# RWKV-6 attention and a leaky-ReLU feed-forward on one core: more transposes by DMA, stores behind the loads, a new written order

## The chip, the core and the metric

The kernel runs on one core of a Trainium2 chip. The metric is device time in microseconds (us), the median of several executions; lower is better. The core has five engines that run side by side and meet only at semaphores: TensorE (PE) multiplies matrices, VectorE (DVE) and GpSimd (POOL) do elementwise work, ScalarE (ACT) does activations and copies, SyncE (SP) issues most of the data transfers (DMAs). A DMA that an engine issues is carried out by 16 DMA engines, and every engine takes its own instructions strictly in their written order.

## The reference

```python
# r, k, v, w: (4, 8, 768, 48) float32;  u: (8, 48)
for t in range(S):
    cur = einsum('bhd,bhe->bhde', u * k[t], v[t])
    y[t] = einsum('bhd,bhde->bhe', r[t], state + cur)
    state = w[t][..., None] * state + einsum('bhd,bhe->bhde', k[t], v[t])
x = y.transpose(0, 2, 1, 3).reshape(3072, 384)
h = x @ w_in                      # w_in: (384, 2048)
out = maximum(0.01 * h, h) @ w_out  # w_out: (2048, 384), out: (3072, 384)
```

The first part is a linear attention with a decaying state; the second is a feed-forward on its 3072 output rows.

## The kernel before

**Tiling.** The 4 batches of 768 rows are cut into 24 chunks of 128 rows. A chunk n goes through these steps, whose names are used below:

- four loads `ld` of w, k, r and v (192 KB each, SP, line 516), of which w is logged on ACT (`decay`);
- `cum` on PE: the running sum of the logs (L737, L742), then `ci` on DVE and two exponentials on ACT;
- two products, r and k each times an exponential, into one tile `rk` (`product`);
- `turn`: the transpose of `rk` into `rkT`. For chunks outside `TDMA` it is 2 times 4 PE transposes (L441) with one PSUM copy each on DVE or ACT; for chunks in `TDMA` it is one DMA transpose that SP issues (L431);
- `scores` on PE (L787), masked on DVE (L459); `outer` (L798) and the new state s (L479), which takes the decayed old state sb (POOL or DVE, `shrink`);
- `bonus`: ru, ruk (POOL or DVE), a reduction dg (DVE), and vs = v times dg (POOL or DVE);
- `intra` on PE (L817, L822), the sum y on DVE (L490), and `finish`: the transpose of y into `xT`, again by 3 PE transposes (L504) and a copy, or by one DMA transpose (L496).

The first four chunks are done two at a time (`pair`). The feed-forward of a chunk is 4 steps `up` (12 matmuls each, L860), 4 activations g on ACT (L907), 4 steps `down` (4 matmuls each, L928), a copy o out of PSUM (ACT or DVE) and a store of 192 KB (L968). The feed-forward weights are loaded in 16 pieces (L363) and cast to bf16 on DVE, ACT and POOL.

**Buffers.** Inputs and raw weights share a ring `in` of 11 tiles of 128 x 1536 floats, taken in turn; output tiles come from a ring `o` of 4. Attention scores use two PSUM banks (`se`, `so`), the `up` steps two (`hp`), the `down` steps two (`op`).

**Order.** Nothing is scheduled at run time. The kernel lists about 1060 steps with an engine, a duration and the steps they wait for, and `Plan.order` replays them to find an order in which they are written into the engines' queues. The string `EARLY` names every step by number, with a letter where a step goes to another of its allowed engines. In each engine's queue its order is binding; DMA steps it ranks only, so the replay may move a transfer past others. The constant `TDMA = range(12, NCH)` says which chunks are transposed by DMA. During the first 24 us of the replay, gaps on PE are filled with matmuls on zeros (L991).

Of the kernel before, what the change touches and what calls it, by code (L numbers as in the profile page):

```python
# [2 lines left out]

# [9 lines left out]
AX = mybir.AxisListType  # L13


class Plan:
# [23 lines left out]
    def order(self):  # L40
        n = len(self.eng)
        users = [[] for _ in range(n)]
        left = [len(d) for d in self.deps]
        for i, d in enumerate(self.deps):
            for j in d:
                users[j].append(i)
        ready_at = [0.0] * n
        start, done = [None] * n, [0.0] * n
        free = {e: 0.8 for e in self.ENGINES}
        coming = {e: [] for e in self.ENGINES}  # L50
        ready = {e: [] for e in self.ENGINES}
        dma_free = 0.0
        flying = []
        for i in range(n):
            if not left[i]:
                heapq.heappush(coming[self.eng[i]], (0.0, i))
        events = [(0.8, e) for e in self.ENGINES]
        heapq.heapify(events)
        count = 0
        while events:  # L60
            now, e = heapq.heappop(events)
            if free[e] > now + 1e-9:
                continue
            while coming[e] and coming[e][0][0] <= now + 1e-9:
                _, i = heapq.heappop(coming[e])
                heapq.heappush(ready[e], (self.pri[i], i))
            if not ready[e]:
                if coming[e]:
                    heapq.heappush(events, (coming[e][0][0], e))
                continue  # L70
            _, i = heapq.heappop(ready[e])
            start[i] = now
            count += 1
            free[e] = now + self.dur[i] * (1.8 if e == "PE" and now < 8 else 1)
            if self.wire[i] is None:
                done[i] = free[e] + self.LAT[e]
            else:

                flying = [x for x in flying if x[0] > free[e]]
                while sum(x[1] for x in flying) + self.rows[i] > 3300:  # L80
                    free[e] = max(free[e], flying.pop(0)[0])
                dma_free = max(dma_free, free[e]) + self.wire[i]
                done[i] = dma_free + 1.7
                flying.append((done[i], self.rows[i]))
            heapq.heappush(events, (free[e], e))
            for j in users[i]:
                left[j] -= 1
                same = self.eng[j] == e and self.wire[i] is None
                ready_at[j] = max(ready_at[j], free[e] if same else done[i])
                if not left[j]:  # L90
                    f = self.eng[j]
                    heapq.heappush(coming[f], (ready_at[j], j))
                    heapq.heappush(events, (max(ready_at[j], free[f]), f))
        assert count == n, (count, n)
        self.start, self.done = start, done
        return sorted(range(n), key=lambda i: (start[i], i))


class Ring:
# [7 lines left out]
    def take(self):  # L107
        self.n += 1
        k = self.n % len(self.tiles)
        old, self.steps[k] = self.steps[k], []  # L110
        return Use(self.tiles[k], old, self.steps[k])

# [14 lines left out]
def kernel(  # L127
# [11 lines left out]
    nc = tc.nc  # L139
    B, H, S, D = r.shape  # L140
    L = 128
    C = S // L
    NCH = B * C
    NP = H // 2
    DM = H * D
# [6 lines left out]
    TDMA = range(12, NCH)  # L152
# [4 lines left out]
    PWIRE, WIRE, WWIRE = 1.53, 1.15, (1.12, 1.12)  # L157
# [4 lines left out]
    EARLY = """  # L162
        0 4 2 1 3 5 8 58 7 13 6 61 12 32v 36 17 11 16 22 33 120 14 21 30 19 37 18 20 24 15 59 10a 23 26
        9 27 31v 28 40 25 60 29a 38 41a 51 34 39 63 44 53 114 62 42 116 45 65a 66 118 121 64 67 122 46
        35 43 71 68 124 47 126 52 74 73 69 96 48 70 128 76 49 75p 72 136 50v 132 79 115a 78 54 91 80 81
        117 130 83 55 77p 82v 56 84a 721 119 134 92 57 85 722 723 86v 138 87 123a 93 95 725 724 97 125p
        98v 727 726 146 127p 729 99 728 88v 100 129 94 731 89 730 102 137p 140 732 733 101 735 133 148
        90 103 734 131 107 736 104 741 135p 144 109 105 742 106v 139a 142 747 108 737 147 150 110 738
        152 141p 178 743 111 153 112 748 304 744 162 113v 754 167 166 155 168 145v 749 154 753 156 750
        143p 149 739 158 163v 179 157p 755 740 759 164 756 180 160 159 182 762 760 184 209 306 745 763v  # L170
        161 185 765 764 746 151v 169 181 187 165v 751 199 761 189p 198 186 170 171 766 752 172 768 302
        173 757 208 188 174 758 192 210 200v 770 193 774 175 183a 239 194v 190 176 775 767 191a 195v 769
        211 177 196 201 779 197 202 212 237 777 780 203 214 771 224 271 778 215 204 217 781 225v 253 303
        772 783 216 205 219p 270 787 782 218 206 784 226 220 213 222 238 241 207v 790 227 221 223 229
        243 269 285 788 232 244 228 789 301 785 230 245 794 786 231 286 773 793 240 246 247 791 795 248p
        334 287 257 801 254v 258 792 259 796 333 273 255 233 251 317 797 275 234 272 249 252 804 276 318
        305 235 250 807 277 256v 397 289 810 290 236 260 279 278 422 799 811v 242a 280p 307 262 261 800
        366 802 264 337 281 319 815 803 291 335 308 805 282a 274 263 322 808 396 309 320 310 311 265 283
        321 288 798 806 818 266 367 284 339 312p 267 395 821 809 340 292 268v 353 341 824 349 365 294
        354 342 813 825v 350 776 313 295 293 814 816 479 344p 314a 296 315 829 343 817 476 323 297 351  # L180
        316 819 408v 368 399 381 324 820 298 832 409 369 423 326 835 327 299 345 382 371 300 410 822 420
        346a 372 827 823 383 325 336 347 386 433 373 830 328 374 375 329 826 831 355 838 449 376 385 836
        828 448 425 348v 839 401 330 370 843 837 402 812 481 331 846 424 384 332v 404 356 338v 477 844
        403 352 359 451 480 357 833 405 406p 845 398 379 360 426 834 850 358 387 452 840 841 427 851 421
        361 380v 377 429 849 362 438 407 437 378 428 852 842 430 388 450 363 853 847 389 453a 454 411
        505 390 400a 857 848 455 860 364 863 465 431 434 854 456 533 855 457 391 435 466 459p 856 858
        436v 432 871 859 392 412 461 506 458 393 864 394 415 462 478 482 413 865 414 874 416a 463 861
        483 464 504 872 862 439v 417 485 866 418 494 487p 869 493 559 484 440 867 441 870 419 517v 877
        873 558 880 444 518 460 885 443 881 489 888 519 507 508 486 875 490 442 510 532 878 876 511 467
        445 491 879 891 492v 521 488 894 562 522 446 534 886 513 895v 512 515p 469 883 887 472 468 514  # L190
        495 884 892 447 470 509a 899 520 516 893 471 889 868 536 584 473 890 538 902 474 642 539 496 497
        550 905 499 540 475 545 908 549 542 541 896 900 498 583 546 909 564 500 897 901 543p 565 524 898
        547 501 523 906 566 527 567 903 526 560 907 569p 913 502 904 916 882 644a 503 525 911 544 528
        919 585 551 912 922 535 587 917 923 927 568 611 918 571v 914 925 572v 915 589 529 926 573 920
        590 586 552 530 601 921 941 554 531 596 592 928 553 561 591 930 537 613 600 548v 929 933 593 944
        615 670 594 936 570 588a 617 597v 931 937 934 932 598 555 574 938 935 563v 939 595 556 599 942
        910 940 618 557 576 947 624 943 924 672v 612 945 629 619 639 950 620 621 946 948 614 579a 575
        949 602 955 578 628 958 951a 577 961 580 964 581 952 953 965a 582 604 956 954 607 625 667 603
        622 957 959 606 630 962 623 643 960 626 641 645 969 605 963 640 627 972 646 608 616v 647 970 609
        657 648 967 610 971 632 975 697 671 635 656 978 968 658v 669 631 979a 973 634 652 696 983 974  # L200
        649 986 633 650p 668 673 653v 976 981 674 977 651 636 654 675 989 637 708 676 992 966 684 677
        685 638 982 660 680 984 993 695 997 709v 980 655 985 994 987 698 663 681 990 678 988 1000 686v
        991 679 659 1003 682 661 683 1006 662 998 699 1007 995 999 710 1008 701 664 996 702 1004 665 713
# [824 lines left out]
```

## Time and profile before

| | us |
|---|---|
| median of 8 runs | 186.35 (185.99 to 187.03) |
| the profiled execution | 187.03 |
| its span, first to last instruction | 184.9 |
| PE busy / DVE / ACT / POOL | 175.9 / 123.1 / 121.5 / 93.6 |
| mean share of the 16 DMA engines on the queue of the transfers | 85.8% |
| granted TensorE clock | 0.997 |

The profile is of one execution, which was the slowest of the eight. Busy time of PE counts a matmul from its start to a modelled end, and matmuls overlap, so the distance between the starts of consecutive matmuls is the better measure of how fast PE runs. "In 40 slices" means that the span is cut into 40 equal parts, and each digit is the busy share of a part in tenths. SPq rows are the time in which SP issues a transfer, not the transfer itself.

### The profile page before, as it was taken

Reading aid. Unit: us, or ns where it says so; the run is one execution under the profiler, and the core shown is the slowest. Engines: PE = TensorE matmul, PEld = TensorE weight load, DVE = VectorE, ACT = ScalarE, POOL = GpSimd, SP = SyncE. Lnnn points to the kernel's source line nnn. Section 1 sums busy time; section 2 is a strip of 40 time slices with the busy share of each in tenths; the row PEclk is TensorE's granted clock in tenths of the full one; section 3 lists DMA queues with packets and bytes.
Section 4 is the critical chain, followed back from the end, with each engine's and each line's share of the span. In section 5 each row is a group of like instructions: output and inputs, shape, how many; then the busy total and the mean of one; then the engine's idle time right before and its main releaser. Section 6 shows DMA issues by size and latency. Waiting matters only on the chain.

```text
span 184.9 us, 6227 instructions
## 1 busy us (share of the span) xinstructions
PE 175.9 (95%) x2579; PEld 136.9 (74%) x2583; DVE 123.1 (67%) x237; ACT 121.5 (66%) x263; POOL 93.6 (51%) x129
## 2 busy tenths in 40 slices
PE   7987789999999999999999999999999999999992
PEld 2465687777788697788688787886968777877882
DVE  2488585368678877987868778657648589775000
ACT  2784965665786987798958586667657645652660
POOL 7987582552376778787365666313516157220000
PEclk9999999999999999999999999999999999999998
DMA  5999999988989799979997998778986979941202
GB/s 145 261 282 312 350 330 274 264 158 211 214 169 237 142 222 211 195 188 220 134 199 144 144 197 179 191 143 171 182 199 155 196 150 211 205 104 44 66 4 85
DMA packets 120239, 34.62 MB, mean 187 GB/s; under 512 B 109842, under 2 KB 120211, under 8 KB 120211
## 3 DMA queue, kind: packets, MB, share of 16 engines
q1 hardware_dynamic: 120208, 34.22, 85.8%
q8 instruction: 20, 0.33, 0.7%
q14 instruction: 9, 0.07, 0.1%
q10 hardware_dynamic: 2, 0.00, 0.0%
HBM read 25.17 MB, written 4.72 MB: 162 GB/s over the span
## 4 chain that ended last, share of the span: by engine, by line
PE 77%; SPq 11%; DMA 7%; DVE 1%; issue 1%; ACT 1%; POOL 1%; DVEq 0%
PE op L928 31%; PE hp L860 31%; SPq L363 6%; SPq L516 5%; DMA in<-in_moe_w_out_dram 4%; PE se L787 3%; DMA in<-in_r_dram 2%; PE yp L822 2%; PE cp L737 2%; PE yp L817 2%; PE yp L798 2%; PE so L441 1%; PE yp L504 1%; PE se L441 1%; PE cp L742 1%
## 5 line engine op out<-in xcount | busy, mean ns | idle before, releaser
L907 ACT ACTIVATE g<-hp 128x512 bf16<-128x512 f32 x96 | 56.8, 596 | 34.4 <-PE hp L860 32.6
L860 PE MATMUL hp<-xT,w_in_b 128*128 128x128 bf16 x1152 | 76.1, 219 | 1.5 <-ACT w_in_b L329 0.8
L860 PEld LDWEIGHTS <-w_in_b 128*128 128x128 bf16 x1152 | 67.4, 98 | 6.5 <-ACT w_in_b L329 1.2
L928 PE MATMUL op<-w_out_b,g 128*128 128x384 bf16 (+1 forms) x380 | 71.4, 324 | 0.2 <-DVE w_out_b L331 0.2
L928 PEld LDWEIGHTS <-g 128*128 128x128 bf16 x392 | 34.8, 98 | 18.0 <-DVE w_out_b L331 0.3
L334 POOL TENSOR_TENSOR ru<-in,ub 128x384 f32<-128x384 f32 x19 | 19.2, 1012 | 13.3 <-DMA in<-in_r_dram 11.4
L334 POOL TENSOR_TENSOR vs<-in,dg 128x384 f32<-128x384 f32 x19 | 16.5, 875 | 16.1 <-DVE dg L416 8.4
L334 POOL TENSOR_TENSOR rk<-in,ek 128x384 bf16<-128x384 f32 x15 | 15.2, 1015 | 14.2 <-ACT ek L393 12.8
L490 DVE TENSOR_TENSOR y<-yp,vs 128x384 bf16<-128x384 f32 x24 | 13.3, 554 | 12.9 <-PE yp L822 9.3
L334 POOL TENSOR_TENSOR ru<-ru,in 128x384 f32<-128x384 f32 x15 | 15.6, 1045 | 6.0 <-DMA in<-in_k_dram 4.4
L334 POOL TENSOR_TENSOR sb<-s,a 128x384 bf16<-128x384 f32 x13 | 11.3, 868 | 9.9 <-DVE s L479 4.7
L459 DVE TENSOR_TENSOR m<-se,maskb 128x512 bf16<-128x512 f32 x20 | 13.7, 684 | 3.2 <-PE so L787 2.9
L459 DVE TENSOR_TENSOR m<-so,maskb 128x512 bf16<-128x512 f32 x20 | 13.7, 683 | 3.0 <-PE so L787 3.0
L383 ACT ACTIVATE lw<-in 128x384 bf16<-128x384 f32 x24 | 12.3, 519 | 3.7 <-DMA in<-in_w_dram 3.7
L752 DVE TENSOR_TENSOR ci<-cp,lw 128x384 f32<-128x384 f32 x20 | 11.0, 552 | 4.2 <-PE cp L742 4.0
L334 DVE TENSOR_TENSOR rk<-in,cp 128x384 bf16<-128x384 f32 x22 | 12.0, 547 | 2.3 <-ACT cp L393 1.9
L416 DVE TENSOR_REDUCE dg<-ru 128x8 f32<-128x384 f32 x24 | 13.0, 544 | 0.2
L329 ACT COPY o<-op 128x384 f32<-128x384 f32 (+1 forms) x16 | 7.5, 471 | 6.5 <-PE op L928 5.1
L479 DVE TENSOR_TENSOR s<-yp,sb 128x384 f32<-128x384 f32 x14 | 7.7, 553 | 5.2 <-PE yp L798 5.2
L393 ACT ACTIVATE cp<-cp 128x384 f32<-128x384 f32 x22 | 10.5, 478 | 0.6 <-DVE ci L752 0.3
L393 ACT ACTIVATE ek<-ci 128x384 f32<-128x384 f32 x20 | 10.4, 518 | 0.4 <-DVE ci L752 0.2
L775 ACT ACTIVATE a<-cp 64x4 f32<-64x4 f32 x34 | 5.7, 167 | 4.2 <-DVE ci L752 2.0
(125 smaller groups left out, 225.4 us busy)
## 6 DMA issues: line engine op xcount, KB each, us to landing
out_dram<-o SPq DMA_DIRECT2D x23, 192.0 KB, 2.9
in<-in_w_dram SPq DMA_DIRECT2D x20, 192.0 KB, 4.2
in<-in_r_dram SPq DMA_DIRECT2D x20, 192.0 KB, 4.1
in<-in_k_dram SPq DMA_DIRECT2D x20, 192.0 KB, 4.0
in<-in_v_dram SPq DMA_DIRECT2D x20, 192.0 KB, 4.0
in<-in_moe_w_in_dram SPq DMA_DIRECT2D x8, 384.0 KB, 7.6
in<-in_moe_w_out_dram SPq DMA_DIRECT2D x8, 384.0 KB, 7.4
in<-in_w_dram SPq DMA_DIRECT2D x2, 384.0 KB, 5.0
```

Source lines behind the costliest of these rows:

```text
L334: (nc.vector if e == "DVE" else nc.gpsimd).tensor_tensor(out=o, in0=a, in1=b, op=ALU.mult)
L363: "SP", 0.45, lambda part=part, src=src: nc.sync.dma_start(out=part, in_=src), pri,
L383: lambda: nc.scalar.activation(out=lw.t[:, :, 0:D], in_=wn.t, func=AF.Ln),
L393: "ACT", 0.5, lambda: nc.scalar.activation(out=out.t[:], in_=i, func=AF.Exp, scale=scale),
L416: lambda: nc.vector.tensor_reduce(out=dg.t[:], in_=ru.t[:], axis=AX.X, op=ALU.add),
L459: lambda par=par: nc.vector.tensor_tensor(out=m.t[:, par], in0=gt(sc[par].t), in1=mask.unsqueeze(1).to_broadcast([128, NP, 128]), op=ALU.m ...
L490: lambda: nc.vector.tensor_tensor(out=y.t[:], in0=hd(yp.t[:, 0:DM]), in1=vs.t[:], op=ALU.add),
L516: "SP", 0.45, lambda: nc.sync.dma_start(out=view(use), in_=src), P0 + 0.1 * i,
L752: lambda: nc.vector.tensor_tensor(out=ci.t[:], in0=hd(cp.t[:, 0:DM]), in1=lw.t[:, :, 0:D], op=ALU.add),
L860: nc.tensor.matmul(hp.t[:, a * N : (a + 1) * N], lhsT=w_in_b[:, t, (j + a) * 128 : (j + a + 1) * 128], rhs=xT[:, t, c0 : c0 + N], start=(a ...
L907: lambda hp=hp, g=g, j=j, J=J, N=N: nc.scalar.activation(out=g.t[:, j : j + J, 0:N], in_=hp.t[:, 0 : J * N].rearrange("p (a n) -> p a n", ...
L928: nc.tensor.matmul(t[:, 0 : n1 - n0], lhsT=g.t[:, j, off : off + 128], rhs=w_out_b[:, j, n0:n1], start=(j == 0), stop=(j == NJ - 1))
```

## The change

The change does six things.

1. The first 230 steps keep their order on every engine. From there on a new string `ORDER` gives the order of all steps; it is binding for transfers too, and `Plan.order` no longer chooses, it only reckons times for the PE fillers. 70 steps change engine, among them 7 loads and 6 stores that now leave from ACT instead of SP.
2. r and k are transposed by DMA from chunk 9 (before from 12), y from chunk 8 (before from 12). This removes 24 PE transposes of r and k with 6 copies, and 12 of y with 4 copies; it adds 3 DMA transposes of `rk` and 4 of y.
3. The copies o of chunks 4 to 23 go into parts of the input tiles 6 to 10 (four outputs to a tile), each of which is used once. Chunks then take their inputs from 6 tiles in a circle, not from 11. In the new order 12 more of the stores than before come after the last load.
4. In the last chunk the `down` matmuls of the left 256 columns and of the right 128 columns are done in two passes (`quarters`).
5. POOL's vs runs as two instructions of 4 heads each (`by_heads`) from chunk 4 on; the w_in casts read and write in an order of 128 columns at a time (`even`).
6. Planned durations are edited; these act through the number of fillers alone, since the order is written out.

```diff
-    TDMA = range(12, NCH)
+    TDMA = range(9, NCH)
+    YDMA = range(8, NCH)
+    OLATE = 21
...
-    EARLY = """
-        0 4 2 1 3 5 8 58 7 13 6 61 12 32v 36 17 11 16 22 33 120 14 21 30 19 37 18 20 24 15 59 10a 23 26
...
+    ORDER = """
+        0 4 2 1 3 5 8 58 7 6 13 61 32v 36 12 17 11 16 22 33 120 14 21 30 19 37 18 20 24 15 59 10a 23 26
...
+    pair_slots = iter((0, 1, 2, 3))
+    weight_slots = iter((4, 5, 6, 7, 8, 9, 10, 0))
+    chunk_slots = cycle((1, 2, 3, 4, 5, 0))
...
+    def out_tile(ch):
+
+        if ch < 4:
+            return o_r.take()
+        slot, i = divmod(ch - 4, 4)
+        use = in_r.use(6 + slot)
+        return View(use, use.t[:, i * DM : (i + 1) * DM])
...
+        def queue(e):
+            return nc.sync if e == "SP" else nc.scalar
+
...
+        def even(t, which):
+
+            return t if which else t.rearrange("p t (a f) -> p a t f", a=2)
...
+        def by_heads(e, o, a, b, parts):
+            for i in range(parts):
+                hs = slice(i * H // parts, (i + 1) * H // parts)
+                times(e, o[:, hs, :], a[:, hs, :], b[:, hs].unsqueeze(2).to_broadcast([128, H // parts, D]))
...
-                "POOL", 0.92,
-                lambda e: times(e, vs.t[:], vn.t, dg.t[:].unsqueeze(2).to_broadcast([128, H, D])),
-                P0 + 2, reads=[vn, dg], writes=[vs], deps=[vl, s_dg], DVE=0.84)
+                "POOL", 0.88,
+                lambda e: by_heads(e, vs.t, vn.t, dg.t, 2 if e == "POOL" and P0 >= 40 else 1),
+                P0 + 2, reads=[vn, dg], writes=[vs], deps=[vl, s_dg], DVE=0.68)
...
-            if n in TDMA:
+            if n in YDMA:
...
-                "SP", 0.45, lambda: nc.sync.dma_start(out=view(use), in_=src), P0 + 0.1 * i,
-                writes=[use], wire=wire, rows=1024, deps=[cums[n - AHEAD]] if n >= AHEAD else [])
+                "SP", 0.62, lambda e="SP": queue(e).dma_start(out=view(use), in_=src), P0 + 0.1 * i,
+                writes=[use], wire=wire, rows=1024, deps=[cums[n - AHEAD]] if n >= AHEAD else [],
+                **({"SP": 0.62, "ACT": 0.47} if n >= 4 else {}))
...
-            slot = in_r.take()
+            slot = in_r.take(next(chunk_slots))
...
+        def quarters(op, g, off, which):
+            for part, q in which:
+                t, n0, n1 = last_parts(op)[part]
+                for j in range(q * NJ // 4, (q + 1) * NJ // 4):
+                    nc.tensor.matmul(
+                        t[:, 0 : n1 - n0], lhsT=g.t[:, j, off : off + 128], rhs=w_out_b[:, j, n0:n1],
+                        start=(j == 0), stop=(j == NJ - 1))
...
-                    o = o_r.take()
+                    o = out_tile(ch)
...
-                        lambda o=o, ch=ch: nc.sync.dma_start(
+                        lambda e, o=o, ch=ch: queue(e).dma_start(
                             out=rows[ch], in_=o.t[:]),
-                        5, reads=[o], deps=[s_o], wire=0.55, rows=128)
+                        5 if ch >= OLATE else 300, reads=[o], deps=[s_o], wire=0.55, rows=128, SP=0.48, ACT=0.47)
```

The two orders, decoded into step names for the transfers of chunks 9 and 10 and of the last chunks (`T` is a DMA transpose of `rk`, `yT` of y, `st` a store, `@A` issued from ACT):

```
before: ... ldk13 T12 ldr14 ldk16 st8 ldk17 T13 ldr16 ldr15 ldw16 ldk18 yT12 ldw18 T14 ...
before: ... ldw23 st17 st18 ldv23 T22 st19 yT21 T23 st20 yT22 yT23 st21 st22 st23L st23R
after:  ... ldk14@A ldv13 ldv10 T9 ldw14 yT8 T10 ldr12 ldv15 ldv14 T11 yT9 ldw15 ldk15 ldr13 ldv12 T12 yT10 ...
after:  ... ldk23 ldv21 T21 st17@A T22 yT20 st2 st3 st10 st7 st11 st13 st0 st9 st18@A st4 st15 yT21 T23 st19@A st20 yT22 yT23 st21 st23L st22@A st23R
```

## The prediction

> **What bounds the kernel now.** I read the page's busy rows first, then the busy time by stretches, then the chain of work that ended last, and last the instructions of PE in order of time.
>
> ```profile
> PE 175.9 (95%) x2579; PEld 136.9 (74%) x2583; DVE 123.1 (67%) x237; ACT 121.5 (66%) x263; POOL 93.6 (51%) x129
> ...
> PE   7987789999999999999999999999999999999992
> ```
>
> PE is busy from the sixth slice (28 us) to the end. The stretches say the same: between 43 and 158 us nothing but PE is full, and the mean DMA share is near its end too.
>
> ```profile
> 43.00:85.00 42.00, 42.00 (x599) 33.49 (x598) 34.50 (x64) 32.56 (x77) 29.30 (x34) 1.00 0.93 197
> 85.00:158.00 73.00, 72.93 (x1024) 57.49 (x1022) 53.59 (x97) 48.95 (x109) 34.99 (x38) 1.00 0.91 178
> 158.00:182.00 24.00, 23.67 (x334) 19.63 (x332) 8.65 (x16) 12.45 (x24) 1.66 (x2) 1.00 0.38 77
> ```
>
> The columns after the first sum are PE, PEld, DVE, ACT, POOL, clock, DMA share, GB/s. A busy PE need not be a PE at its peak, so I take the chain, where the pieces follow without a hole:
>
> ```profile
> 97.67 1.34 PE hp L860 x24
> 99.01 0.20 PE yp L822 x8
> 99.21 0.65 PE op L928 x4
> 99.86 0.67 PE hp L860 x12
> ...
> 146.79 0.58 SPq L516
> 147.42 4.59 DMA in<-in_r_dram
> 152.10 0.56 DVE rk L334
> ```
>
> An `up` step takes 0.67 us and a `down` step 0.65 wherever they stand. The last three lines are one of the few places after 43 us where the chain leaves PE, for a load; PE itself waited only 0.23 us there. To size what PE loses in all, I give each PE step the median distance from its start to the next step's. From the `up` step at 42.9 us to the end of the last matmul at 181.7 that is 137.3 us, against 138.6 really gone by: all stalls of that stretch come to 1.4 us. So the end is set by how much work PE has, once the weights are there. Before 30 us PE stands still for 9.6 us (matmul starts again), for loads and weight casts.
>
> Here a rule of the Trainium skill speaks against the change. "Perfetto Trace Analysis", section "Identifying the Most-Contended Engine", calls the busy share of matmuls a bad measure and wants that of the weight loads. That is 74%, which would leave PE a quarter of the span in reserve, and work taken off PE would bring 0. By the distances of starts it brings its full length. The distances are measured here, and I go by them.
>
> **The change, part by part.**
>
> *PE transposes removed.* Their cost is the distance to the next step:
>
> ```profile
> 77.25 0.33 PE L504 MATMUL yp<-ident,y 128*128 128x128 bf16 x3
> 77.42 0.39 PE L441 MATMUL se<-ident,rk 128*128 128x128 bf16 x4
> 77.64 0.33 PE L737 MATMUL cp<-lw,trev 128*128 128x384 bf16 x1
> ```
>
> 0.17 us for the three of y, 0.22 for four of r or k. Six groups of four (chunks 9 to 11) and four groups of three (8 to 11): 6 x 0.22 + 4 x 0.17 = 2.0 us, all on the path. The ten copies that go with them (6 on ACT, 4 on DVE) free 3.2 and 1.6 us of engines that are not the bound: 0.
>
> *DMA transposes added.* The 12 of each kind in the trace:
>
> ```profile
> L431 SPq DMA_TRANSPOSE rkT<-rk x12: 1232/1554/3566, 85.5 to 163.4; - x12
> ...
> DMA to landing us min/median/max: 3.1/4.1/5.6
> ```
>
> A transpose of y takes 1.20 to issue and 2.9 to land. A chunk's `rkT` thus comes some 4 us after the products, where the PE way needs 0.39 on PE and 0.58 for the copy at best. "VectorE: DVE Perf Modes", section "The three transpose paths", makes it worse: 1309 ns for a 128x128 block by DMA against 390 on TensorE, with the rule to take TensorE where the result may go to PSUM. For the 36 blocks moved that would be 36 x 0.92 = +33 us if it stood in line. The trace has eight blocks of `rk` landing in 4.1 us, so half a microsecond each, and what they cost depends on what is put between. Adding up PE's durations over the decoded new order gives, from `cum` to `scores`, 12.7, 12.0 and 11.8 us for chunks 9, 10 and 11; chunks that go by DMA now have 8.3 to 21 there, with hardly a stall. From `intra` to the first `up`, chunks 8 to 11 get 5.5 to 8.6; chunks 22 and 23 live on 4.5 and 5.0 now. Covered: 0. Without that cover chunk 9 alone would hold PE by up to 3 us.
>
> *Transfers moved.* By packets in the trace, a load takes 1.0 us of the 16 engines (80.5 us for 80 loads' worth), a pair of transposes 1.70 + 0.64 (28.1 us for 12 pairs), a store 0.55. Seven transposes add 3 x 1.70 + 4 x 0.64 = 7.7 us to the whole. Ahead of the last load, however, stand 12 `rk` and 12 y transposes where there are 10 and 9 now (+3.4 + 1.9), and 7 stores instead of 19 (-6.6): the last load comes after 1.3 us less of transfers than now. SP issues 7 transposes more (3 x 1.55 + 4 x 1.20 = 9.4 us) and 13 other transfers fewer (about 8): it ends even. Ten stores stand in a row ahead of chunk 21's y and chunk 23's r, k; at 0.55 each they fill 5.5 us that PE needs for its steps up to `intra` of chunk 21, about 9 us after the stores can begin. Cost 0; without that cover, up to 1 us.
>
> *ACT as an issuer.* Thirteen issues. The one DMA that ACT issues now took 0.53 us, a load on SP 0.43 to 3.1[...]. 13 x 0.5 = 6.5 us on ACT, which loses 2.8 us of other work and is 66% busy. Behind an issuing ACT stand the g activations, and behind these PE, with two `hp` banks as cover. From below -0.3 (SP's queue moves on earlier), from above four issues of 1.5 us past a cover of 0.7 = +3. I take 0, near the one row.
>
> *Six input tiles for eleven.* A load of chunk n must wait for vs and the products of chunk n-6 on SP, with all later transfers behind it. Before 85 us SP now waits for buffers about 6 us in all. I expect 4 us more, not on PE's path as long as the transposes of `rk` keep their lead: -0 to +2, taken 0.
>
> *POOL's split, casts, last chunk, fillers.* 14 vs in two halves: nothing to 0.2 us each (a small POOL memset takes 0.10), 1.4 us in all, POOL is idle half of the time. The w_in cast on DVE (0.95 us, one of them) may change by 0.3 either way: -0.3 to +0.3. The last chunk's matmuls are the same in sum (2.7 us); its last-but-one store is now chunk 22's 192 KB from ACT instead of 64 to 128 KB from SP: 0 to +0.3. The 15 fillers may become more or fewer, each 0.43 us, in a stretch where PE idles: -0.4 to +0.4. Together taken as +0.1.
>
> *Sum.* -2.0 + 0.1, and for new small stalls +0.1, since the products and transfers are timed less evenly: -1.8. The profiled execution took 187.03; that makes 185.2. It was the slowest of eight, 0.7 above the median of 186.35, where the same difference gives 184.5.
>
> **The rivals.**
>
> *Transfers become the bound (slower).* In the new order chunk 17's `rk` transpose has 85 us of transfers from the end of the w load of chunk 5 (64 loads, 9 + 8 transposes, a store, at the prices above), and a PE without stalls wants it at 126. From 33 us, with some 3 us of weights still in flight and 1.7 for landing, 88 us remain: a pace of 0.97 is needed. Between 44 and 85 us SP got 35 loads and 6 stores through in 40.9 us, a pace of 0.94, its 6 us of waits included, 1.09 without. At 0.94 the transpose is 2.4 us late, and PE, whose `scores` are next in line, stops. Every transpose after it is then late as well:
>
> ```profile
> 85.53 3.57 SPq L431 DMA_TRANSPOSE rkT<-rk  x1
> ...
> 92.11 2.01 SPq L431 DMA_TRANSPOSE rkT<-rk  x1
> ```
>
> shows that the first DMA transpose can hold SP for 3.6 us, and the packets of some transposes run four times longer than others. With one such hold more (1.5 us over the usual) the lag is 3.9 us: -2.0 + 3.9 gives 188.2. For it: SP is one queue and the tiles are six. Against it: after 85 us SP spends about 10 of each 25 us waiting for data, not for transfers, so that the transfers are not the limit there. It decides from a pace below 0.95.
>
> *Part of the gain is eaten.* Single late products (DVE gets 2.3 us of work net, just where it is 80% busy) or ACT's issues stall PE 1.5 to 2 us: 186.1.
>
> *The early order isn't really unchanged.* The v load of chunk 9 stands two places later on SP, and the fillers are counted anew. If the first stretch gains or loses one load's 1 us, the result is 183.5 or 185.5. ACT's long issues belong on the far side: 187.
>
> **How the numbers follow.** PE bound as reckoned, 183.3 to 185.5: 0.58. Part eaten, 185.5 to 186.9: 0.14, of which 0.04 is still faster by over 0.3%. Transfers bound: 0.21, 187 to 190. ACT's issues or six tiles beyond the cover: 0.07, 187. A run of this kernel can tell about 0.3% (0.56 us) from no change. Faster 0.62, same 0.09, slower 0.29. The range for 8 in 10 goes from 183.2 to 187.9, which leaves out the worse half of the transfers' case and the best of the first; the likeliest case alone is 183.3 to 185.5.
>
> **What would show it.** Right: about 36 fewer PE matmuls, the `up` steps still back to back from 43 us on, no L787 or L860 with idle time before it for a transpose, the last matmul near 180. Transfers as the bound: PE waits of 0.5 us and more ahead of `scores` of chunks 12 to 19, and the chain going through SPq L431 and SPq L516. ACT: long ACTq rows with g right behind. I'd be wrong on the sizing if PE's start distances lengthened without any wait.

## The result, and the profile after

The changed kernel takes 191.05 us (median of 11 runs, 189.4 to 195.6) against 186.35 before (185.86 to 187.09): 1.0214 times the time, with a 95% interval of 1.0194 to 1.0234. The prediction was 184.5 us, faster. The ratio leaves out four runs of 193 to 196 us, in which TensorE's mean clock was 0.978 or 0.979 where it was 0.991 or 1.0 in the others; what lowers the clock is part of what follows, but none of these four has a profile.

The profiled execution took 190.67 us (span 188.8). From its page, the row of PE and that of TensorE's clock:

```profile
PE 178.3 (94%) x2549; PEld 138.2 (73%) x2552; DVE 124.6 (66%) x243; ACT 113.4 (60%) x245; POOL 96.9 (51%) x145
...
PEclk9999999999999999999997899999999999999999
```

The trace has 30 matmuls fewer, and yet PE is busy for 2.4 us more. The 7 and 8 in the clock's row, at 99 to 108 us, are the reason: part of the work ran at half speed. The busy times by stretches (after the first sum: PE, PEld, DVE, ACT, POOL, clock, DMA share, GB/s):

```profile
43.00:85.00 42.00, 41.64 (x589) 32.85 (x587) 35.61 (x68) 29.18 (x67) 30.92 (x40) 1.00 1.01 183
85.00:158.00 73.00, 70.87 (x968) 56.04 (x967) 53.58 (x99) 42.56 (x96) 37.52 (x49) 0.98 0.98 183
158.00:182.00 24.00, 22.75 (x327) 18.99 (x325) 8.33 (x15) 12.11 (x23) 0.83 (x1) 1.00 0.40 126
```

Before, the middle stretch held 72.93 us of PE work at clock 1.00; now 2.1 us of it are empty and the mean clock is 0.98. PE's last matmul ends at 185.1 us in place of 181.7, with the `up` step that the prediction counted from at 42.6 in place of 42.9: 142.6 us for what took 138.8. The view of waits names the two largest holes, and who stood behind the second:

```profile
ACT g L924 <- DMA out_dram<-in: 2.3, 1, 2.3
PE se L796 <- DMA rkT<-rk: 1.9, 1, 1.9
PE op L949 <- ACT g L924: 1.4, 2, 1.2
```

**First hole.** SP's own instructions and PE's, in order of time (start, duration; idle time before in brackets):

```profile
90.05 0.58 SPq L524 DMA_DIRECT2D in<-in_r_dram  x1
90.68 1.40 SPq L524 DMA_DIRECT2D in<-in_w_dram  x2
92.18 1.72 SPq L504 DMA_TRANSPOSE xT<-y  x1
94.00 0.53 SPq L524 DMA_DIRECT2D in<-in_k_dram  x1
94.63 2.00 SPq L439 DMA_TRANSPOSE rkT<-rk  x1
...
98.32 0.78 PE L869 MATMUL hp<-xT,w_in_b 128*128 128x128 bf16 x11
100.96 0.23 PE L796 MATMUL se<-rkT 48*128 48x128 bf16 x1 [1.86 <-DMA rkT<-rk]
```

The products of chunk 13 were ready at 89.5. Its transpose (the row at 94.63) stood in SP's queue behind the w loads of chunks 16 and 17, y's transpose of chunk 11 and the k load of chunk 18, whose data were first used at 123.4. It was issued 5.1 us after it could have been, took 6.3 us to land, and PE stood still for 1.86 us. It is none of the added transposes: before, chunk 13 went by DMA too. It was issued at 92.11 us there (a row that the prediction shows), and its `scores` came 8.4 us later, without a wait:

```profile
100.46 0.23 PE L787 MATMUL se<-rkT 48*128 48x128 bf16 x1
```

In the changed kernel the clock then went to half for 3.41 us; these are the two steps of the clock's record on either side of 101.45 us:

```profile
98.04:101.45 3.41, 1.55 (x29) 1.22 (x27) 2.29 (x5) 1.72 (x5) 1.53 (x2) 1.00 1.24 196
101.45:104.86 3.41, 3.41 (x27) 2.73 (x26) 2.52 (x5) 1.08 (x2) 3.13 (x4) 0.50 0.84 163
```

The second has PE busy throughout, with half the matmuls for the time: 1.7 us lost with no wait shown.

**Second hole.** ACT and PE around 160 us:

```profile
156.95 0.48 ACT L328 COPY in<-op 128x384 f32<-128x384 f32 x1 [2.65 <-PE op L949]
159.31 0.34 ACTq L985 DMA_DIRECT2D out_dram<-in  x1
159.69 1.08 ACT L924 ACTIVATE g<-hp 128x512 bf16<-128x512 f32 x2 [2.27 <-DMA out_dram<-in]
160.34 0.82 PE L949 MATMUL op<-w_out_b,g 128*128 128x384 bf16 x4 [1.25 <-ACT g L924]
```

The copy o of chunk 18 was done at 157.4. ACT then stood until 159.25 before it could issue the store: in the trace the store waits for the semaphore that SP's store of chunk 10, issued at 157.00 in the row of ten, had used before it. g and the `down` step behind it were late by as much.

With the median distances of PE's steps, as in the prediction, all stalls from 43 us on come to about 7.3 us: 1.9 for chunk 13's scores, 1.7 for the half clock, 1.5 for ACT's store, and some 2.2 in small pieces of up to 0.4.

### The profile page after: what moved, and what is told of

It reads as the page before. It is cut to its first block, busy times and chain, and to the rows that moved or that the text cites. A ratio compares the mean times of both kernels' runs of the same rounds, so it can differ in the third digit from the quotient of the medians.

```text
span 188.8 us, 6154 instructions
## 1 busy us (share of the span) xinstructions
PE 178.3 (94%) x2549; PEld 138.2 (73%) x2552; DVE 124.6 (66%) x243; ACT 113.4 (60%) x245; POOL 96.9 (51%) x145
## 4 chain that ended last, share of the span: by engine, by line
PE 56%; DMA 18%; SPq 12%; DVE 5%; ACT 4%; issue 2%; ACTq 1%; DVEq 0%
PE hp L869 23%; PE op L949 22%; SPq L524 5%; SPq L366 5%; DMA in<-in_moe_w_out_dram 5%; DMA in<-in_w_dram 4%; DMA rkT<-rk 3%; DMA in<-in_v_dram 3%; DMA xT<-y 2%; PE se L796 2%; ACT g L924 2%; PE yp L831 1%; PE yp L826 1%; DMA out_dram<-in 1%; ACTq L524 1%
## 5 line engine op out<-in xcount | busy, mean ns | idle before, releaser
L869 PE MATMUL hp<-xT,w_in_b 128*128 128x128 bf16 x1152 | 77.9, 221 | 1.3 <-ACT g L924 1.0
L869 PEld LDWEIGHTS <-w_in_b 128*128 128x128 bf16 x1152 | 68.7, 99 | 7.1 <-issue 2.2
L949 PE MATMUL op<-w_out_b,g 128*128 128x384 bf16 x368 | 70.9, 328 | 1.4 <-ACT g L924 1.4
L949 PEld LDWEIGHTS <-g 128*128 128x128 bf16 x368 | 33.1, 98 | 18.0 <-ACT g L924 1.3
L333 POOL TENSOR_TENSOR ru<-in,ub 128x384 f32<-128x384 f32 x21 | 22.4, 1070 | 11.8 <-DMA in<-in_r_dram 8.0
L333 POOL TENSOR_TENSOR vs<-in,dg 128x192 f32<-128x192 f32 (+1 forms) x32 | 19.0, 615 | 11.0 <-DVE dg L424 11.0
L333 POOL TENSOR_TENSOR rk<-in,ek 128x384 bf16<-128x384 f32 x11 | 11.3, 1023 | 1.5 <-ACT ek L396 1.4
L330 POOL CAST vb<-in 128x384 bf16<-128x384 f32 x14 | 7.3, 528 | 8.5 <-DMA in<-in_k_dram 3.5
L328 ACT COPY in<-op 128x384 f32<-128x384 f32 (+1 forms) x11 | 5.2, 468 | 8.7 <-PE op L949 5.1
```

Of the source, the lines that this page charges most:

```text
L333: (nc.vector if e == "DVE" else nc.gpsimd).tensor_tensor(out=o, in0=a, in1=b, op=ALU.mult)
L869: nc.tensor.matmul(hp.t[:, a * N : (a + 1) * N], lhsT=w_in_b[:, t, (j + a) * 128 : (j + a + 1) * 128], rhs=xT[:, t, c0 : c0 + N], start=(a ...
L949: nc.tensor.matmul(op.t[:, 0:DM], lhsT=g.t[:, j, off : off + 128], rhs=w_out_b[:, j, :], start=(j == 0), stop=(j == NJ - 1))
```

## The experiments

Four theories. **A**: the transposes by DMA are late because of their places in SP's one queue, and a wait of PE's can halve the clock besides. **B**: ACT as a second issuer does the harm. **C**: the small edits do. **D**: all transfers together are the limit. Orders are given in the names of the steps (`ld` load, `st` store, `T` transpose of r and k, `yT` of y, `@A` issued from ACT). Ratios are to the kernel before, run on the same chip; differences between kernels are taken from them (1% is 1.86 us) unless medians are named. Waits of PE's in the text are read from the distances of its starts, and come out 0.1 to 0.2 us longer than in the view of waits.

| run | us, median | ratio, 95% interval |
|---|---|---|
| e1 T of chunk 13 early | 188.60 | 1.0127 (1.0106 to 1.0148) |
| e2 all issued by SP | 186.97 | 1.0029 (1.0011 to 1.0046) |
| e3 small edits alone | 185.89 | 0.9987 (0.9978 to 0.9996) |
| e4, e7, e8 longer waits on e3 | 186.20, 187.38, 190.76 | 1.0006, 1.0053, 1.0206 |
| e5 SP's queue by deadline | 184.57 | 0.9917 (0.9900 to 0.9934) |
| e6 stores on SP | 187.78 | 1.0111 (1.0070 to 1.0153) |
| e9 one load moved | 185.93 | 0.9954 (0.9923 to 0.9985) |
| e10 e5, loads on ACT | 186.43 | 0.9988 (0.9966 to 1.0009) |
| e11 e5 again | 185.01 | 0.9932 (0.9908 to 0.9955) |
| e12 e5, y of chunk 8 on PE | 183.92 | 0.9881 (0.9866 to 0.9895) |
| e13 e12, loads on ACT | 183.77 | 0.9858 (0.9833 to 0.9884) |
| e14 e12, stores on ACT | 185.25 | 0.9923 (0.9894 to 0.9952) |

### e1: one transpose issued earlier

```diff
-  ... T12 yT10 ldr14 ldw16 ldw17 yT11 ldk18 T13 ...
+  ... T12 yT10 ldr14 T13 ldw16 ldw17 yT11 ldk18 ...
```

> The changed kernel with one step moved: SP issues the DMA transpose of chunk 13's r and k right after the r load of chunk 14, ahead of the w loads of chunks 16 and 17, y's transpose of chunk 11 and the k load of chunk 18, behind which it stood. In the changed kernel it was issued 5.1 us after its products and landed 1.9 us too late for PE, and TensorE's clock went to 0.5 for 3.4 us right after. Theory A (the transpose stands too late on SP's one queue, and the wait halves the clock): no wait ahead of chunk 13's scores, no half clock at 101 us, 191.05 - 1.9 - 1.7 = 187.5 us; if the later loads run into the same thing at another chunk, 188 to 190. Theory B (the second queue is what delays: transfers and stores issued by ACT): the wait there goes too, but since ACT's issues remain, half clocks or waits of the same size turn up elsewhere: 190 to 191.

188.60 us, 1.6 less by the ratios, within A's second range. In the profiled run there is no wait ahead of chunk 13's scores and the clock is 1.0 throughout, but PE now waits 0.9 us at an `up` step of chunk 11 and 1.9 us at chunk 14's outer product, which waits in e2 too.

### e2: everything on SP

```diff
-  "ACT": thirteen loads and stores
+  "SP": the same, at the same places of the order
```

> The changed kernel with its thirteen ACT-issued loads and stores issued by SP, at the same places of the order. Theory B (ACT as the second issuer costs): the 1.4 us at the down step of 160 us, the 0.5 us at the up step of 120 us and part of the 1.9 us at chunk 13's scores go, 191.05 - 2 to -3 = 188 to 189 us. Theory A (no reserve in SP's queue): SP gets 13 issues more, some 8 us, and chunk 13's transpose is still late: 190.5 to 192.

186.97 us, 3.4 less by the ratios, at a clock of 0.997 or more in all 18 runs. That is more than B asked for, and A, which expected 190.5 or more, missed. The wait at chunk 13's scores is still there, as A says, but with 0.8 us in place of 1.9. Its transpose was issued at much the same time (94.40) and landed in 5.0 us; in the changed kernel and in e6, where ACT issued the w load of chunk 18 0.6 us behind it, it took 6.3 and 6.6. The next wait:

```profile
106.41 0.67 DVE L333 TENSOR_TENSOR ru<-in,ub 128x384 f32<-128x384 f32 x1 [1.36 <-DMA in<-in_r_dram]
107.60 0.33 PE L807 MATMUL yp<-vb,rk 128*128 128x96 bf16 x4 [1.05 <-DVE y L498]
```

DVE waits for the r load of chunk 16; the sum y of chunk 13 is behind that on DVE; chunk 14's outer product needs the bank that this sum empties. The load went out at 101.7 us, though its input tile had been free since 77.3: it was SP's order that held it, not the six tiles.

### e3: the small edits alone

```diff
-  TDMA = range(9, NCH); YDMA = range(8, NCH); six input tiles in a circle; the new order
+  TDMA = YDMA = range(12, NCH); 11 input tiles, o ring of 4; the order of before
```

> The kernel before with the changed kernel's small edits alone (vs in two parts on POOL, the casts in strips, the last chunk in four passes, the planned durations): 11 input tiles, o ring, all transfers on SP, transposes by DMA from chunk 12, and the order of before written out. Theories A and B both: the edits are neutral, 186.0 to 186.8 us. Theory C (the split on POOL, which took 1.11 us for 0.56, or the fillers cost): over 187.

185.89 us, 0.1 below the lower end of A's and B's range and 0.4 under before: C falls. POOL's vs in two parts takes 1.03 us on the mean (1.10 in the changed kernel) for 0.88 and is hidden.

### e5: SP's queue by deadline

```diff
-  ... T12 yT10 ldr14 ldw16 ldw17 yT11 ldk18 T13 ldv17 ldr15 ldw18 yT12 ldr17 ldr16 T14 ...
+  ... ldr14 ldw16 yT10 T12 ldw17 ldk14 T13 yT11 ldv17 ldr15 ldk15 ldw18 yT12 ldr16 T14 ldr17 ...
```

> e2_all_sp (all transfers on SP) with SP's queue from 66 us on in another order: at each point the step that is ready and whose first user comes earliest, less 4.7 us for a transpose of r and k, 3.4 for one of y, 3.2 for a load; stores behind all that. All other engines keep their order, so the work is that of the changed kernel. Theory A (what is wrong with the change is the order of SP's queue, not the transposes by DMA, the six tiles or the small edits): the waits at chunk 13's scores (0.8 us in e2) and at chunk 14's outer product behind the late r load of chunk 16 (1.2) go, and the 1.6 us of PE's shorter work come through: 186.97 - 2.0 to -3.0 = 184.0 to 185.0. Theory D (the transfers as a whole are the bound: share of the DMA engines 0.97 to 1.03 from 43 to 158 us): another order only moves the wait to another chunk: 186.5 to 187.5.

184.57 us, 2.1 under e2 and inside A's range; D falls. The same transfers in another order give:

```profile
85.00:158.00 73.00, 73.00 (x1037) 58.11 (x1036) 56.29 (x104) 45.76 (x103) 38.80 (x50) 1.00 0.99 184
...
PE hp L869 <- DMA xT<-y: 0.8, 1, 0.8
```

PE is full for 73 us at a DMA share of 0.99. A share near 1 was no proof that transfers were the limit. One wait of size is left, for y of chunk 8 at 79 us.

### e6: the stores on SP, the loads still on ACT

```diff
-  st12@A st14@A st17@A st18@A st19@A st22@A
+  st12 st14 st17 st18 st19 st22
```

> The changed kernel with its six ACT-issued stores issued by SP at the same places of the order; the seven loads stay on ACT. If the stores tie ACT to SP's burst of stores: the 1.5 us at the down step of 160 us go and nothing else, 189.5. If the ACT-issued loads are the larger part of e2's 4.1 us, most of that is still there: 189 to 190. If the stores are all of it: 187.

187.78 us, 1.9 less than the changed kernel by the ratios (3.3 by the medians), where 1.5 was expected. The hole at 160 us is gone. The wait for chunk 13's transpose is not: it was 2.3 us in the profiled run, longer than in the changed kernel, and yet the clock stayed whole. The stretches, cut at the steps of that run's clock record:

```profile
96.02:99.43 3.41, 1.93 (x23) 1.36 (x21) 3.11 (x6) 2.14 (x6) 1.53 (x2) 1.00 1.19 187
99.43:102.84 3.41, 2.69 (x43) 2.33 (x44) 2.22 (x4) 1.24 (x3) 2.03 (x3) 1.00 0.72 136
```

The wait is spread over two steps; neither falls under half. Two of the six runs had a clock of 0.99 and took 189.5 on the mean, the other four 187.6: with such a scatter, 1.9 bears the expected 1.5 out and no more.

e6 and e2 differ by the seven loads alone, and e2 is 0.8% (1.5 us) faster. So in this order the loads on ACT cost time too. The waits for `rkT` in e6 and in e2, and the changed kernel's chain over the k load of chunk 22, with g and an `up` step behind it (0.3 us late there, 0.9 in e6):

```profile
PE se L796 <- DMA rkT<-rk: 2.4, 2, 2.2
PE se L796 <- DMA rkT<-rk: 1.0, 2, 0.7
...
116.63 1.79 ACTq L524
...
119.36 0.52 ACT g L924
119.93 0.83 PE hp L869 x12
```

That the w load of chunk 18 lengthens the landing of chunk 13's transpose is read from three profiles (6.3 and 6.6 us with it on ACT, 5.0 without); no run moves this load alone.

### e4, e7, e8: a wait of chosen length

```diff
e4  -  up19.1 dn19.0 up19.2 up19.3 dn19.1 sc21
e4  +  up19.1 sc21 dn19.0 up19.2 up19.3 dn19.1
e7  +  sc21 up19.1 dn19.0 ...
e8  +  Y20 sc21 dn18.2 dn18.3 out21 up19.1 dn19.0 ...
```

> The kernel of e3_small_edits with one PE step moved: the scores of chunk 21 stand one up step and three quarters of a down step earlier, ahead of the first down step of chunk 19, so that PE reaches them some 2 us before their DMA transpose (issued at 151.4, landing near 155.5) and waits; nothing else differs, and the work is the same. If a wait of about 2 us halves the clock for the next 3.4 us: 2.0 + 1.7 = 3.7 us over e3_small_edits, 190.1. If a wait costs its own length alone: 188.4.

> As e4_wait_2us, with the scores of chunk 21 another up step and a third of a us earlier: in e4 PE waited 1.2 us there, in one stretch, and the clock stayed whole; now it should wait about 2.1 us, as long as at chunk 13's scores in the changed kernel. If such a wait halves the clock for 3.4 us: mean clock 0.99, 185.89 + 2.1 + 1.7 = 189.7. If not: 188.0. If it depends on where the wait falls: both, from run to run.

> As e4 and e7, with the scores of chunk 21 right behind the inter-chunk product of chunk 20, 1.3 us earlier than in e7, which waited 1.2 to 1.5 us at full clock. PE should now wait some 2.9 us in one stretch. The clock records of the runs so far change only at steps of 3.41 us, with another phase in each run, and the one step after 43 us at half clock (changed kernel, 101.4 to 104.9 us) followed a step in which PE was busy for 46%; steps with 57, 64 and 65% changed nothing. If a step under half busy halves the next: a wait of 2.9 us leaves some step under half in nearly 9 of 10 phases: most runs at a mean clock of 0.99, 185.89 + 2.9 + 1.7 = 190.5, the rest 188.8. If a wait costs its own length alone: 188.8 in all runs, clock 1.0.

e4 waited 1.2 us and e7 1.4, not 2: the transpose lands earlier than I reckoned. Neither halved the clock at that place; they cost 0.3 and 1.2 us over e3. e8 waited 2.5 us:

```profile
151.69:155.10 3.41, 1.23 (x14) 0.80 (x15) 0.95 (x2) 1.13 (x4) 3.13 (x5) 1.00 0.85 191
155.10:158.51 3.41, 3.41 (x24) 2.43 (x23) 2.36 (x6) 0.60 (x1) 0.00 (x0) 0.50 0.65 176
```

A step with PE busy for 36%, and the next at half clock. 190.76 us, as expected for a wait that halves: five of six runs had clocks of 0.982 to 0.991 and took 190.6 to 191.7 us, 190.9 on the mean, the sixth 1.0 and 189.15. One wait, no transfer changed: the clock's share is about 1.8 us, by five runs against one.

### e9 and e10: one load moved; loads back on ACT

```diff
e9   -  ldr12 ldv14 ldv15 yT8 T10 ldw15 ldr13 T11
e9   +  ldr12 ldv14 yT8 T10 ldw15 ldr13 ldv15 T11
e10  -  ldk12 ldw13 ldk13 ldk14 ldw18 ldv22 ldk22
e10  +  ldk12@A ldw13@A ldk13@A ldk14@A ldw18@A ldv22@A ldk22@A
```

> e5_by_deadline with one load moved on SP: the v load of chunk 15 goes behind the r load of chunk 13, so that the transpose of y of chunk 8, for which PE waited 0.95 us at the up step of 79 us, is issued 0.7 to 0.9 us earlier. Theory A: that wait shrinks to 0.1 to 0.3, 183.7 to 184.0. If the wait only moves to the next transpose: 184.5.

> e5_by_deadline with the seven loads that the changed kernel issues from ACT put back there, between the same ACT steps as in the changed kernel; stores on SP, the rest of SP's queue as in e5. Theory B (a second issuing engine costs by itself): the load of k of chunk 22 stood 1.8 us in ACT's queue ahead of an exponential and g, and the up step of chunk 14 waited 0.4 to 0.9 us: 185.0 to 185.8. If ACT's issues only hurt together with a late SP queue: 184.3 to 184.8.

Both missed and settle nothing by their times: 184.65 to 189.9 us and 185.2 to 189.2, on a chip where before ran up to 187.7 as well. In both profiles PE waits longer for y of chunk 8 (1.7 and 2.3 us). SP was behind already: the transpose of chunk 9's r and k left it at 74.0 and 72.7 us where e5 has 70.9, and y's of chunk 8 at 76.7 and 78.2 where e5 has 74.9. Why these two runs were late is open. They do narrow down the clock's threshold:

```profile
77.78:81.19 3.41, 1.76 (x21) 1.01 (x20) 2.70 (x5) 1.22 (x3) 3.23 (x6) 1.00 0.66 121
79.50:82.91 3.41, 1.83 (x36) 1.76 (x35) 0.61 (x2) 0.89 (x2) 2.93 (x4) 1.00 0.79 151
```

The first is e9, busy for 52%, and half clock after it; the second e10, 54%, and full clock.

### e11 and e12: y of chunk 8 back on PE

```diff
-  YDMA = range(8, NCH);   ... y8 yT8 ...
+  YDMA = range(9, NCH);   ... y8, ytp8 behind up7.2 (PE), xT8 (DVE)
```

> e5_by_deadline once more, as the base for e12 on the same chip, and because e9 and e10, which differ from it by one moved load and by seven loads on ACT, spread over 185 to 190 us with waits of 1.7 and 2.3 us for y's transpose of chunk 8 where e5 had 0.95. If e5's six runs were typical: 184.4 to 185.2, little spread. If the transposes' landing times vary by chip or by run and e5 met a quiet one: 185 to 187, with a spread over 2 us.

> e5_by_deadline with the transpose of chunk 8's y put back on TensorE (three PE transposes behind the second up step of chunk 7, the copy on DVE): PE has 0.17 us more to do, and the wait of 0.95 us at the up step of 79 us, 1.7 in e9 and 2.3 in e10, goes. Theory A (a transpose by DMA pays where there is room between its product and PE, and the one of chunk 8 has none): 0.8 us under e11 where e11 waits as e5 did, more where it waits longer, and less spread. If the room was not the matter: 0.2 over e11.

e11 confirms e5 (185.01, spread 1.5 us), and e12 on the same chip takes 183.92, 1.1 less by the medians, with a spread of 0.5. It beats before and the changed kernel. Its page's PE row and chain by engine, and its stretches:

```profile
PE 175.8 (96%) x2555; PEld 136.0 (75%) x2555; DVE 124.4 (68%) x244; ACT 113.8 (62%) x245; POOL 96.8 (53%) x145
...
PE 80%; SPq 11%; DMA 7%; issue 1%; DVE 0%
...
43.00:85.00 42.00, 41.89 (x591) 33.05 (x589) 35.55 (x71) 29.50 (x68) 30.48 (x40) 1.00 1.00 188
85.00:158.00 73.00, 73.00 (x1044) 58.33 (x1042) 56.29 (x103) 45.86 (x103) 38.67 (x50) 1.00 0.94 186
```

In the changed kernel PE had 56% of the chain, transfers (DMA and SPq) 30%; here it is 80 and 18, much as before (77 and 18).

### e13 and e14: what ACT as an issuer costs by itself

```diff
e13  -  ldk12 ldw13 ldk13 ldk14 ldw18 ldv22 ldk22
e13  +  ldk12@A ldw13@A ldk13@A ldk14@A ldw18@A ldv22@A ldk22@A
e14  -  st12 st14 st17 st18 st19 st22
e14  +  st12@A st14@A st17@A st18@A st19@A st22@A
```

> e12_y8_on_pe, whose PE hardly waits, with the seven loads that the changed kernel issues from ACT put back there between the same ACT steps; SP's queue otherwise as in e12. Theory B (a second issuing engine costs by itself): ACT's issues of 0.2 to 1.8 us stand ahead of exponentials and g, the up step of chunk 14 waits 0.4 to 0.9 us: 184.5 to 185.3. If they hurt only together with a late SP queue: 183.7 to 184.2.

> e12_y8_on_pe with the six stores that the changed kernel issues from ACT put back there between the same ACT steps; the other stores stay on SP, behind all loads and transposes. Theory B: a store of ACT waits, as in the changed kernel, for a store of SP's burst that had its semaphore before it, g behind it is late, and a down step near 157 us waits 1 to 1.5 us: 185 to 185.5. If that was an accident of the changed kernel's places: 183.7 to 184.2.

Here the loads cost nothing: 183.77, where B expected 184.5 or more. ACT as an issuer of loads does no harm by itself; the 1.5 us of e6 against e2 come with SP's late queue. The stores cost 1.2 us against e13, run on the same chip (four runs of 184.6 to 185.6), and two more runs at clocks of 0.98 took 189.6 and 189.9. The profile is of one of these, so where the four lose their 1.2 us it does not show:

```profile
PE hp L869 <- DMA xT<-y: 2.6, 1, 2.6
...
129.91:133.32 3.41, 1.59 (x22) 1.07 (x22) 2.29 (x5) 1.06 (x3) 0.83 (x1) 1.00 1.07 191
133.32:136.74 3.42, 2.66 (x33) 2.40 (x33) 0.32 (x1) 1.17 (x4) 2.15 (x4) 0.50 0.69 137
```

Here the wait is at another place than B said. y's transpose of chunk 16, issued at 128.50 (in e13 0.9 us earlier), was used at 134.08, 5.6 us later; in e13 it was 3.45, without a wait. Just then the store of chunk 14, issued from ACT, runs on the second queue: from 128.3 to 131.3 the transposes' 256-byte packets took 24 to 42 ns on the mean, where they took 18 to 22 in e13. The Trainium skill ("DMA: Bandwidth & Descriptors", section "Issuing engines are not separate DMA queues") has it that transfers from different engines run on the same 16 DMA engines and interleave, and that a second issuer saves only issue time; these packets agree. That the store is what made this transpose late is read from one run and not shown by an experiment.

## Why the prediction was wrong, step by step

By the ratios the changed kernel is 4.0 us slower, where 1.8 us less was expected. Two terms taken at 0 failed, and one was missing. In the order of the runs, with all transfers on SP 3.4 us come back (e2), with SP's queue sorted 2.1 more (e5), and with y of chunk 8 on PE 1.0 more (e12 against e11), which ends 2.2 us under before (e5 and e11 are one kernel on two chips, 0.3 us apart).

*PE bound; removed transposes, -2.0 "all on the path".* Right. From the `up` step to the last matmul's end e3 takes 138.5 us and e12 137.0 (e13 136.8). With the 0.17 us of the y transpose that e12 puts back, that is 1.7 of the 2.0, with e12's remaining small waits in it. Reading PE's reserve from the weight loads, which would have made it 0, does not hold here.

*DMA transposes added, "Covered: 0".* This step failed first. I compared about 12 us from `cum` to `scores` with the 8.3 to 21 of the chunks that went by DMA already. But a transpose starts when SP gets to it, and what covers it is the distance from its issue to the `scores`. For chunk 13 that was 4.5 us of PE work where 6.3 were needed, because of four transfers ahead of it in SP's queue. In before's trace the distances from issue to `scores` are 4.2 to 9.7 us with landings of 3.1 to 5.6: there was little to spare there either, and I had the starts on SP in hand. I also looked at chunks 9 to 11 alone, whose transposes are new. The new order took the cover from chunk 13, which went by DMA before (8.4 us there). I worked out what "without that cover" would cost and gave it to chunk 9 (up to 3 us); it came at chunk 13, and as 1.9 us.

*The clock.* No term of the sum had it. Right behind that wait stood a half clock for 3.41 us: 1.7 us. My sign for "wrong on the sizing", start distances of PE that lengthen without a wait, is what it looks like.

*ACT as an issuer, taken 0 from -0.3 to +3.* This step failed too. In the order of the change the thirteen issues cost 3.4 us with what the clock lost (e2): 1.9 for the six stores (e6; 1.5 in the profile) and 1.5 for the seven loads. In the sorted order the loads cost 0 (e13) and the stores 1.2 (e14). The one row that I went by was a single load; it could not show a store that waits for another's landing, nor a late transpose in SP's queue that, as the three profiles suggest, lands later still beside ACT's load.

*Ten stores in a row, "cost 0; without that cover, up to 1 us".* I looked at y of chunk 21 and the transpose of chunk 23 behind them. Those were in time; the cost was on ACT, whose store waited for one of the ten.

*Six input tiles, 0; small edits, +0.1.* Right: the late load of chunk 16 had its tile 24 us before (e2), and e3 is 0.4 below before. The split of vs costs 0.15 us each in e3 and 0.22 in the changed kernel, about my 0.2, and is hidden.

*First rival, transfers as the bound, from chunk 17 on, 188.2.* On the right side of the result, but by another mechanism. Its sign, waits of 0.5 us and more ahead of `scores` in chunks 12 to 19, came at chunk 13 alone. e5 and e12 move the same loads and stores at a DMA share of 0.94 to 0.99 with PE full; what was short was not the pace but the order.

*The three transpose paths* (the Trainium skill, "VectorE: DVE Perf Modes", section "The three transpose paths": 1309 ns by DMA, 390 on TensorE; the rule to take TensorE stands in the same page's section "Rules for kernel authors"), taken as +33 us for standing in line, and my 0: neither. Where there is room between the product and its use, a transpose by DMA gave nearly its whole PE time (e12); where there was none, for y of chunk 8, it cost 0.95 to 2.3 us of waiting to save 0.17 (e11 against e12: 1.1).

## What to carry to other kernels

Before work is handed to a queue, measure the cover from where the queue will issue it, with everything that stands ahead of it, to the first use; the distance from the input's birth says nothing. A queue served in order wants its entries sorted by who needs them first: with all of them on SP the same transfers took +0.3%, so sorted -0.8%, and with one transpose given back to PE -1.2%. A second issuing engine is no free room: the thirteen issues from ACT were the step from +0.3% to +2.1%, and a store there can wait for another store's landing with an engine's work behind it. And a wait on a bound PE of about half a clock step or more may cost the clock's loss on top.

## What the runs showed of the hardware

The clock's record changes only at steps of 3.413 us. In every profiled run the times between changes are whole multiples (26, 1 and 25 steps in the changed kernel, 51 in before), with a phase that differs from run to run. After the start-up, a step with PE busy for 36, 45, 47 or 52% was followed by one at half clock; steps with 54, 57 and 64% were not. Busy time is modelled, so the line between 52 and 54% is rough. Full clock came back after one step in which PE was busy throughout (changed kernel, e8); in e14, where PE was busy for 78% of the first step at half clock, it took two. What brings it back is not shown further. The Trainium skill ("TensorE: Matmul & The Clock Gate", section "HAM oscillation — how this bites in real kernels") asks for no idle gaps over some 3.4 us. By that rule the 1.9 us ahead of chunk 13's scores would have cost 1.9; by the runs it cost 3.6. Waits of 1.7 to 2.5 us halved the clock or did not, as they fell within one step or across two. That fits the scatter of the changed kernel and of e6, 2 us and more, against 0.5 in e12; which runs lost how many steps is known for the profiled ones alone.
